# One decode layer on one core: projections with the activations stationary in four column groups, K loaded in 16 KiB runs, layernorm 2 in rows

## The chip, the cores and the metric

The kernel runs on one core of one Trainium2 chip. The metric is the device time of one execution in microseconds (us). Most executions of a kernel agree within 0.3%, so "faster" is kept for more than 2%; smaller differences can still be told apart when several runs agree. "Span" is the time from the first to the last instruction in the profile; the measured time lies about 1.8 us above it, and one section below is about cases where it lies higher. In the views PE is the matmul engine and PEld its weight loads, DVE and ACT are the vector and the scalar engine, and SP issues most of the DMAs. PSUM is the memory that matmuls write to, and an eviction is the copy out of it. "q1", "q8" and "q14" are the DMA queues as the profile numbers them.

## The reference, cut to what matters

Four rows of width 1024 pass through attention over the last 2048 cached keys, and then through a gated feed-forward block.

```python
# B=4 rows, D=1024, Hq=32, Hkv=4, Dh=128, W=2048 keys, F=3584; all bf16
def _A_ref(x, k_cache, v_cache, wq, wo):
    q = (x @ wq) ...                       # wq 1024 x 4096
    scores = einsum("bhqd,bhkd->bhqk", q, k) * Dh ** -0.5
    o = einsum("bhqk,bhkd->bhqd", softmax(scores), v)
    return o ... @ wo                      # wo 4096 x 1024
def _B_ref(x, w1, w3, w2):
    return (silu(x @ w1) * (x @ w3)) @ w2  # w1, w3 1024 x 3584, w2 3584 x 1024
h  = x + _A_ref(_layernorm(x), ...)
h2 = h + _B_ref(_layernorm(h), ...)
```

Each weight and each cached key is read once and used for four rows: 55.6 MB of loads, little arithmetic.

## The kernel before

All loads are issued in the order of use from one queue, into ten buffers of 16 KiB a partition; each buffer is refilled when its tile has been used.

```python
stream = ctx.enter_context(tc.tile_pool(name="stream", bufs=10))
# ... cut ...
def load_kv(cache, b):                      # K and V: runs of 4 KiB
    kv_t = stream.tile([P, Hkv, NK, Dh], BF16, tag="s")
    nc.sync.dma_start(
        out=kv_t[:], in_=cache[b, :, Sk - W : Sk, :].rearrange("g (p j) d -> p g j d", j=NK)
    )
    return kv_t
# ... cut ...
for kc in range(KC):                        # q: the WEIGHTS are stationary, 4 columns stream by
    wq_t = loaded["wq"][kc // KPC]
    for h in range(Hq):
        nc.tensor.matmul(
            qT_ps[:, h, :],
            lhsT=wq_t[:, kc % KPC, h * P : (h + 1) * P],
            rhs=xnT[:, kc, :], ...
        )
    if kc % KPC == KPC - 1:
        load_next()
# ... cut: K transposes, scores, softmax, P times V; wo, gate and up in the same form as q ...
for fc in range(FC):                        # w2: the activations are stationary, four column groups
    w2_t = loaded["w2"][fc // RPC]
    for j in range(JG):
        nc.tensor.matmul(
            y2_ps[32 * j : 32 * j + B, :],
            lhsT=hgT[:, fc, :],
            rhs=w2_t[:, fc % RPC, j * CG : (j + 1) * CG], ...
        )
res = act.tile([P, CG], BF16)
nc.vector.tensor_copy(out=res[:], in_=y2_ps[:])
# ... cut: four small output DMAs, two each from SP and ACT ...
```

The q, wo, gate and up projections need one matmul for each 128 x 128 block of weights: 256 + 256 + 448 of the kernel's 1716 matmuls. Each matmul is two instructions, a weight load and the matmul.

## Time and profile before

| | before |
|---|---|
| time, median of 4 runs | 141.59 us (141.53 to 141.65) |
| span of the profiled run | 139.9 us |
| loads | 55.58 MB, 4096 packets of 4 KiB for K and V |
| matmuls, and as many weight loads | 1716 |
| last load landed / output issued | 136.20 / 137.13 us |

The page of before, cut: the busy share of PE and of the 16 DMA engines in 40 equal slices (in tenths), what they moved, and the DMA queues with packets, MB and share.

```profile
span 139.9 us, 3709 instructions
PE 81.7 (58%) x1716; PEld 66.6 (48%) x1716; DVE 37.0 (26%) x92; ACT 25.4 (18%) x41; POOL 0.7 (1%) x6
...
PE   0252241469999999900897282938966334834460
...
DMA  5999999999999999999999999999999999999930
GB/s 157 426 422 431 436 431 391 425 412 422 422 415 422 422 418 415 421 432 429 429 417 429 426 439 435 419 430 435 418 431 418 443 406 429 417 431 422 405 132 5
...
q1 hardware_dynamic: 8352, 55.58, 95.2%
q8 instruction: 13, 0.21, 0.5%
...
q14 instruction: 2, 0.02, 0.0%
```

The DMA row is full from the second slice to the last but two. No compute stage leaves a dent in it, not even the K stage, where PE is full (slices 10 to 17). With the same bytes to load, two things are left that can shorten this kernel: faster packets, or a shorter way from the last full slice to the end.

The end of the chain of waits before (start, duration, what):

```profile
89.20 32.24 DMA w_t<-in_B_w_dram
121.44 0.02 issue
121.46 14.74 DMA w_t<-in_B_w_dram
136.20 0.04 issue
136.24 0.41 PE y_ps L398 x4
136.66 0.02 issue
136.68 0.42 DVE res L408
```

After the last piece of w2 has landed only 4 matmuls, one eviction and the output follow. Now the load itself, in windows of half a microsecond (the last two columns are the DMA share and GB/s):

```profile
132.00:132.50 0.50, 0.28 (x8) 0.00 (x0) 0.00 (x0) 0.00 (x0) 0.00 (x0) 0.50 1.02 410
132.50:133.00 0.50, 0.00 (x0) 0.00 (x0) 0.00 (x0) 0.00 (x0) 0.00 (x0) 0.50 0.75 303
133.00:133.50 0.50, 0.00 (x0) 0.00 (x0) 0.00 (x0) 0.00 (x0) 0.00 (x0) 0.50 0.59 234
133.50:134.00 0.50, 0.27 (x8) 0.20 (x11) 0.00 (x0) 0.00 (x0) 0.00 (x0) 0.50 0.52 209
134.00:134.50 0.50, 0.50 (x16) 0.31 (x9) 0.00 (x0) 0.00 (x0) 0.00 (x0) 0.50 0.39 156
134.50:135.00 0.50, 0.28 (x12) 0.02 (x7) 0.00 (x0) 0.00 (x0) 0.00 (x0) 0.50 0.33 127
135.00:135.50 0.50, 0.50 (x8) 0.20 (x8) 0.00 (x0) 0.00 (x0) 0.00 (x0) 0.50 0.32 123
135.50:136.00 0.50, 0.46 (x8) 0.09 (x4) 0.00 (x0) 0.00 (x0) 0.00 (x0) 0.50 0.11 41
```

The share does not fall at once, it falls for 3.5 us: the 16 engines do not end together. The trace also holds a completion event for each engine's part of each load. These are the 16 parts of the last load before, in ns after the first of them (which is at 132.9 us):

```
0 37 87 169 211 274 457 | 1239 1379 1726 1837 | 2888 3091 3094 3097 3300
```

Seven engines end together, four about 1.4 us later, five about 1.5 us later still. On the first wq tile the same 16 parts lie within 0.5 us. The page shows what else these engines carry: 13 "instruction" packets on q8, each 16 KiB and 0.88 to 0.96 us long in the trace, against 0.61 us for a 16 KiB packet of data. The trace does not name the engine of a packet or of a part, so which engine carried which packet is inferred from counts and times.

### The profile page before, as it was taken

The numbers are of one execution on the slowest core, as the hardware profiler recorded it, in microseconds if no ns is written. First come the engines' busy times: TensorE is split into PE (matmuls) and PEld (weight loads), VectorE is DVE, ScalarE is ACT, GpSimd is POOL, SyncE is SP. The second block draws the span as 40 slices with busy tenths as digits, with TensorE's granted clock in tenths as the row PEclk, the third lists the DMA queues.
The fourth block names the chain that finished last, engine by engine and source line by source line (L and its number), as shares of the span: only waits on it lengthen the run. The fifth ranks groups of instructions, "written<-read, shape, count | busy, mean of one in ns | idle before, by whom it ended". The sixth has DMA issues, their size and how long they took to land.

```text
span 139.9 us, 3709 instructions
## 1 busy us (share of the span) xinstructions
PE 81.7 (58%) x1716; PEld 66.6 (48%) x1716; DVE 37.0 (26%) x92; ACT 25.4 (18%) x41; POOL 0.7 (1%) x6
## 2 busy tenths in 40 slices
PE   0252241469999999900897282938966334834460
PEld 0252241467777777500797181917966333712120
DVE  6600000335777777661700310012003000000001
ACT  3000000024566666519100000000004000000000
POOL 2000000000000000000000000000000000000000
PEclk9999999999999999997555555555555555555555
DMA  5999999999999999999999999999999999999930
GB/s 157 426 422 431 436 431 391 425 412 422 422 415 422 422 418 415 421 432 429 429 417 429 426 439 435 419 430 435 418 431 418 443 406 429 417 431 422 405 132 5
DMA packets 8391, 55.82 MB, mean 399 GB/s; under 512 B 548, under 2 KB 564, under 8 KB 5048
## 3 DMA queue, kind: packets, MB, share of 16 engines
q1 hardware_dynamic: 8352, 55.58, 95.2%
q8 instruction: 13, 0.21, 0.5%
q10 hardware_dynamic: 24, 0.01, 0.1%
q14 instruction: 2, 0.02, 0.0%
HBM read 55.58 MB, written 0.01 MB: 397 GB/s over the span
## 4 chain that ended last, share of the span: by engine, by line
DMA 52%; PE 32%; DVE 5%; issue 4%; ACT 2%; SPq 1%; ACTq 0%
DMA w_t<-in_B_w_dram 34%; DMA kv_t<-in_A_k_cache_dram 19%; PE kt_ps L232 12%; PE scores_ps L215 10%; PE OT_ps L275 5%; PE yT_ps L313 4%; DVE PT_sb L267 2%; DVE rmax L246 2%; ACT Pm L251 1%; SPq L75 1%; ACT L251 1%; DVE o_1208 L295 1%; PE o_ps L289 0%; PE pt_ps L264 0%; DVE OT_sb L285 0%
## 5 line engine op out<-in xcount | busy, mean ns | idle before, releaser
L236 ACT CAST kT<-kt_ps 128x512 bf16<-128x512 f32 x32 | 17.4, 589 | 37.0 <-PE kt_ps L232 28.0
L234 DVE CAST kT<-kt_ps 128x512 bf16<-128x512 f32 x32 | 20.8, 687 | 10.5 <-ACT kT L236 6.1
L374 PEld LDWEIGHTS <-w_t 128*128 128x128 bf16 x448 | 15.6, 118 | 10.1 <-DMA w_t<-in_B_w_dram 7.9
L232 PEld LDWEIGHTS <-kv_t 128*128 128x128 bf16 x256 | 17.1, 105 | 6.6 <-DMA kv_t<-in_A_k_cache_dram 3.1
L232 PE MATMUL kt_ps<-ident,kv_t 128*128 128x128 bf16 x256 | 18.4, 231 | 3.0 <-DMA kv_t<-in_A_k_cache_dram 3.0
L215 PE MATMUL scores_ps<-kT,Qm 128*128 128x512 bf16 x64 | 17.0, 392 | 0.0
L188 PE MATMUL qT_ps<-xnT,wq_t 128*128 128x4 bf16 x256 | 7.5, 166 | 12.6 <-DMA wq_t<-in_A_wq_dram 12.6
L188 PEld LDWEIGHTS <-wq_t 128*128 128x128 bf16 x256 | 7.1, 104 | 13.0 <-DMA wq_t<-in_A_wq_dram 13.0
L374 PE MATMUL uT_ps<-hnT,w_t 128*128 128x4 bf16 x224 | 8.1, 173 | 7.4 <-DMA w_t<-in_B_w_dram 7.4
L398 PE MATMUL y_ps<-w_t,hgT 128*4 128x256 bf16 x112 | 7.5, 404 | 8.0 <-DMA w_t<-in_B_w_dram 8.0
L313 PE MATMUL yT_ps<-o_1208,wo_t 128*128 128x4 bf16 x256 | 7.2, 166 | 6.5 <-issue 5.1
L313 PEld LDWEIGHTS <-wo_t 128*128 128x128 bf16 x256 | 7.1, 104 | 6.9 <-issue 6.9
L275 PE MATMUL OT_ps<-PT_sb,kv_t 128*128 128x8 bf16 x256 | 7.4, 168 | 2.9 <-issue 2.2
L398 PEld LDWEIGHTS <-hgT 128*4 128x4 bf16 x112 | 3.5, 104 | 11.9 <-issue 10.1
L374 PE MATMUL gT_ps<-hnT,w_t 128*128 128x4 bf16 x224 | 8.0, 173 | 1.8 <-issue 1.3
L275 PEld LDWEIGHTS <-kv_t 128*128 128x128 bf16 x256 | 7.3, 104 | 3.3 <-issue 3.3
L215 PEld LDWEIGHTS <-Qm 128*128 128x128 bf16 x64 | 5.8, 101 | 4.3 <-issue 0.5
L202 DVE TENSOR_SCALAR Qm<-qT_ps 128x8 bf16<-128x8 f32 x16 | 1.3, 158 | 19.9 <-PE qT_ps L188 19.9
L264 PE MATMUL pt_ps<-Dm,Pm 128*128 128x128 bf16 x16 | 1.9, 311 | 6.6 <-DVE Dm L257 6.6
L345 ACT ACTIVATE rstd_t<-var_t,eps_t 128x4 f32<-128x4 f32 x1 | 0.3, 297 | 28.4 <-DVE var_t L343 28.4
L264 PEld LDWEIGHTS <-Pm 128*128 128x128 bf16 x16 | 1.6, 146 | 7.0 <-ACT Pm L251 7.0
L408 DVE CAST res<-y_ps 128x256 bf16<-128x256 f32 x1 | 0.4, 425 | 15.3 <-PE y_ps L398 15.3
(58 smaller groups left out, 30.1 us busy)
## 6 DMA issues: line engine op xcount, KB each, us to landing
w_t<-in_B_w_dram SPq DMA_DIRECT2D x8, 1792.0 KB, 31.9
wq_t<-in_A_wq_dram SPq DMA_DIRECT2D x4, 2048.0 KB, 7.3
kv_t<-in_A_k_cache_dram SPq DMA_DIRECT2D x4, 2048.0 KB, 32.9
kv_t<-in_A_v_cache_dram SPq DMA_DIRECT2D x4, 2048.0 KB, 23.6
wo_t<-in_A_wo_dram SPq DMA_DIRECT2D x4, 2048.0 KB, 24.3
w_t<-in_B_w_dram SPq DMA_DIRECT2D x6, 1024.0 KB, 27.7
w_t<-in_B_w_dram SPq DMA_DIRECT2D x1, 512.0 KB, 20.1
w_t<-in_B_w_dram SPq DMA_DIRECT2D x2, 256.0 KB, 14.7
```

Of the source, the lines that this page charges most:

```text
L188: nc.tensor.matmul(qT_ps[:, h, :], lhsT=wq_t[:, kc % KPC, h * P : (h + 1) * P], rhs=xnT[:, kc, :], start=(kc == 0 and h == 0), stop=(kc == ...
L215: nc.tensor.matmul(scores_ps[:, n * 512 : (n + 1) * 512], lhsT=Qm[:, bg2, :], rhs=kT_tiles[bg2][:, n * 4 : (n + 1) * 4, :], start=(bg2 == ...
L232: nc.tensor.matmul(kt_ps[:, jj, :], lhsT=k_t[:, g, j, :], rhs=ident[:], start=True, stop=True)
L234: nc.vector.tensor_copy(out=kT[:, jb * JPB : (jb + 1) * JPB, :], in_=kt_ps[:])
L236: nc.scalar.copy(out=kT[:, jb * JPB : (jb + 1) * JPB, :], in_=kt_ps[:])
L246: nc.vector.reduce_max(out=rmax[:], in_=scores_ps[:], axis=AX.X)
L251: nc.scalar.activation(out=Pm[:], in_=scores_ps[:], func=ACT.Exp, bias=nmax[:], scale=1.0, accum_out=rsum[:],)
L264: nc.tensor.matmul(pt_ps[:, jj, :], lhsT=Pm[:, j * P : (j + 1) * P], rhs=Dm[:], start=True, stop=True)
L275: nc.tensor.matmul(OT_ps[:, b, g * REP : (g + 1) * REP], lhsT=v_t[:, g, j, :], rhs=PT_sb[:, j, b * Hq + g * REP : b * Hq + (g + 1) * REP], ...
L313: nc.tensor.matmul(yT_ps[:, dc, :], lhsT=wo_r[:, dc // KPC, dc % KPC, :], rhs=o4[:, h4, r, :], start=(h4 == 0 and r == 0 and dc == 0), sto ...
L374: nc.tensor.matmul(gu_ps[i][:, fc, :], lhsT=w_v[:, fc // RPC, fc % RPC, :], rhs=hnT[:, kc, :], start=(kc == 0 and fc == 0), stop=(kc == KC ...
L398: nc.tensor.matmul(y2_ps[32 * j : 32 * j + B, :], lhsT=hgT[:, fc, :], rhs=w2_t[:, fc % RPC, j * CG : (j + 1) * CG], start=False, stop=(fc ...
```

## The change

The intent was to make PE's work smaller. The four rows of activations become the stationary operand in all projections, the weights stream past, and four column groups of PE work side by side, as in w2 before. For the scores the same is done by head, which asks for K with the heads interleaved over partitions; this gives K runs of 16 KiB. Layernorm 2 moves to the row layout that the new projections leave. The core of the diff (cuts marked):

```diff
-    def load_kv(cache, b):
+    def load_k(b):
+        k_t = stream.tile([P, JK * Dh], BF16, tag="s")
         nc.sync.dma_start(
+            out=k_t[:],
+            in_=A_k_cache[b, :, Sk - W : Sk, :].rearrange("g (pp j) d -> pp g (j d)", pp=PK),
 ... (V stays in runs of 4 KiB; w2 now in tiles of 7 rows, loaded in pieces of 4 and 3)
+    x_q = act.tile([P, CG], BF16)
+    for j in range(JG):
+        nc.scalar.dma_start(
+            out=x_q[QD * j : QD * j + B, :], in_=x_flat[:, j * CG : (j + 1) * CG]
+        )
 ...
-            nc.tensor.matmul(
-                qT_ps[:, h, :],
-                lhsT=wq_t[:, kc % KPC, h * P : (h + 1) * P],
-                rhs=xnT[:, kc, :],
+        for hf in range(CQ // 512):
+            for g in range(JG):
+                c0 = g * CQ + hf * 512
+                nc.tensor.matmul(
+                    q_ps[QD * g : QD * g + B, hf * 512 : (hf + 1) * 512],
+                    lhsT=xnT[:, kc, :],
+                    rhs=wq_t[:, kc % KPC, c0 : c0 + 512],
 ... (wo, gate and up likewise; K by transposes into bf16; scores by head in 32 columns;
      layernorm 2 by statistics of 256 columns, joined by one small matmul; gate over 896 columns)
     res = act.tile([P, CG], BF16)
-    nc.vector.tensor_copy(out=res[:], in_=y2_ps[:])
+    nc.vector.tensor_copy(out=res[:, : CG // 2], in_=y2_ps[:, : CG // 2])
+    nc.scalar.copy(out=res[:, CG // 2 :], in_=y2_ps[:, CG // 2 :])
```

## The prediction

> **What bounds it now.** The 16 DMA engines. The 40 slices show DMA at 9 tenths from slice 2 to the end of slice 38, about 424 GB/s, and the queue table 55.58 MB. The windows view shows no dip in the K phase (413 to 423 GB/s, 26 to 61 us), although PE is the chain there: ten buffers hide it. From 102 us on, every weight tile is waited for (wait view: PE waits 15.5 us for w_t). The chain ends in the last w2 piece, landing at 136.2; then 4 matmuls 0.41, eviction 0.42, output to 139.9.
>
> **The end is ragged.** In the windows view the DMA share falls to 0.75, 0.59, 0.52, 0.39, 0.33, 0.32, 0.11 in half-microsecond steps from 132.5 on. The completion events say why: the 16 parts of one load land 0.5 us apart at first, and 3.3 us apart at the end, in three groups: seven engines 0 to 0.4 us, four 1.2 to 1.9, five 2.9 to 3.3. The groups grow one by one with the 13 instruction packets (queue q8: 16 KiB each, about 0.94 us). A ninth packet, at 97 us, starts the third group: so they look dealt in turn over eight engines, five of which got two. The Trainium skill (DMA: Bandwidth & Descriptors, Queues, rings and completion order) says that each engine goes round between the queues it has work for; the trace agrees, at about 1.4 us lost per packet.
>
> **What the change does.**
> 1. PE instructions. Matmuls fall from 1716 to about 1055 (q 256 to 64, wo 256 to 128, gate and up 448 to 128; K transposes, scores, V, w2 keep their counts), each with a weight load. 3432 instructions for 13 packets is 264 each; 2110 give an estimated 8 packets: no engine should get two. Worth one step of the ragged end: -1.4 us (range 0 to 1.7). On the critical path, because the last load waits for its slowest engine.
> 2. K in 16 KiB runs: 2048 packets of 4 KiB become 512. Packets took 159 ns (4 KiB), 309 (8), 611 (16); landings of 2 MiB tiles were 4.97, 4.90 and 4.86 us apart. Four tiles: -0.45 us, on the path. w2 rows of 8 and 6 KiB cost an estimated +0.05 us.
> 3. Eviction split over DVE and ACT: -0.13 us of 0.42.
> 4. Four extra small x loads: +0.1 us.
> 5. Off the path: the projections (column groups already run side by side: 112 w2 matmuls of 404 ns take 7.5 us), scores with 32 columns, bigger K evictions, row layernorm. They end attention earlier, but the DMA was never starved, so I count 0. The gate's reciprocal grows from 112 to 896 elements a row: 0.85 us to an estimated 6.5, hidden beneath w3's 17 us.
>
> Sum: 141.61 - 1.4 - 0.45 - 0.13 + 0.15 = **139.8 us**; range 138.8 to 141.3. Faster by over 2% (below 138.8): 0.1; within 2%: 0.87; slower: 0.03.
>
> **What would show it.** About 8 instruction packets on q8; last parts at most about 2 us apart instead of 3.3; the DMA share falling over 2 us rather than 3.5; last w2 landing near 134.4. K packets of 16 KiB near 611 ns, tiles 4.86 us apart. PE busy falls a lot and PE's idle time grows by as much. Last wait before the output still DMA.
>
> **What would make it wrong.** Packets dealt otherwise, so that one engine still gets two (then 141). K runs 2 MB apart in a partition's neighbours hitting memory worse than 4 KiB runs (up to +1). Switching between full and column-group matmuls, or strided reads of kT, stretching K by over 10 us, so that buffers come free late and the DMA starves: then slower. Chain at the gate not hidden: +1.

## The result, and the profile after

Before took 141.59 us and after 139.99 us (medians of 4 runs, after from 139.94 to 140.57). The ratio is 0.9897, with a 95% interval from 0.987 to 0.9923. Ratios here are the mean time of one kernel's fast runs over that of the other's of the same rounds, so not quite the ratio of the medians. By the 2% rule this is "the same", but the 1.6 us are well outside the scatter of before.

The page of after, the same lines:

```profile
span 138.2 us, 2365 instructions
PE 75.0 (54%) x1057; PEld 43.4 (31%) x1057; DVE 37.1 (27%) x71; ACT 29.4 (21%) x29; POOL 0.7 (1%) x6
...
DMA  5999999999999999999999999999999999999950
GB/s 154 433 423 436 417 436 436 441 413 432 441 402 409 420 421 416 425 423 430 429 429 417 425 442 424 428 432 428 432 428 432 432 432 413 421 427 430 409 216 2
...
q1 hardware_dynamic: 6960, 55.58, 95.7%
q8 instruction: 8, 0.13, 0.3%
...
q14 instruction: 1, 0.01, 0.0%
```

The end of the chain of waits after:

```profile
121.33 12.97 DMA w_t<-in_B_w_dram
134.29 0.04 issue
134.34 0.41 PE y_ps L448 x4
134.75 0.02 issue
134.77 0.30 DVE res L458
135.07 0.02 issue
135.10 0.27 ACT res L459
```

And the windows at the end of the load:

```profile
131.50:132.00 0.50, 0.15 (x4) 0.10 (x7) 0.00 (x0) 0.00 (x0) 0.00 (x0) 0.50 1.09 434
132.00:132.50 0.50, 0.50 (x12) 0.26 (x5) 0.00 (x0) 0.00 (x0) 0.00 (x0) 0.50 0.87 344
132.50:133.00 0.50, 0.16 (x4) 0.00 (x0) 0.00 (x0) 0.00 (x0) 0.00 (x0) 0.50 0.57 221
133.00:133.50 0.50, 0.42 (x8) 0.23 (x8) 0.00 (x0) 0.00 (x0) 0.00 (x0) 0.50 0.58 221
133.50:134.00 0.50, 0.47 (x8) 0.09 (x4) 0.00 (x0) 0.00 (x0) 0.00 (x0) 0.50 0.28 107
```

The middle of the DMA row is as full as before. The fall at the end takes 2 us instead of 3.5, and the chain says where the time went: the last load lands at 134.29 instead of 136.20 us, 1.91 us earlier, and about 0.17 us are given back between the end of the last matmuls and the output, which was issued at 135.39 us (135.39 - 134.75 = 0.64 us; before 137.13 - 136.66 = 0.47). Together that is the 1.7 us by which the span is shorter. The 16 parts of the last load (the first at 132.46 us):

```
0 90 180 253 346 391 428 | 1175 1480 1489 1562 1572 1716 1783 1809 1840
```

The third group is gone. The first engines end 0.4 us earlier than before (132.46 against 132.9), the last ones 1.9 us earlier. These are two effects, and the experiments take them apart.

### The profile page after: what moved, and what is told of

Read it like the earlier page. It is cut to its first block, busy times and chain, and to the rows that moved or that the text cites. A ratio compares the mean times of both kernels' runs of the same rounds, so it can differ in the third digit from the quotient of the medians.

```text
span 138.2 us, 2365 instructions
## 1 busy us (share of the span) xinstructions
PE 75.0 (54%) x1057; PEld 43.4 (31%) x1057; DVE 37.1 (27%) x71; ACT 29.4 (21%) x29; POOL 0.7 (1%) x6
## 4 chain that ended last, share of the span: by engine, by line
DMA 74%; PE 16%; ACT 5%; SPq 1%; issue 1%; DVE 0%; ACTq 0%
DMA w_t<-in_B_w_dram 55%; DMA k_t<-in_A_k_cache_dram 14%; PE kt_ps L271 10%; DMA wq_t<-in_A_wq_dram 5%; ACT kT L277 5%; PE scores_ps L256 5%; SPq L118 1%; PE y_ps L448 0%; DVE res L458 0%; ACT res L459 0%; SPq L111 0%; ACTq L277 0%
## 5 line engine op out<-in xcount | busy, mean ns | idle before, releaser
L277 ACT COPY kT<-kt_ps 128x1024 bf16<-128x1024 bf16 x16 | 15.9, 1013 | 14.5 <-PE kt_ps L271 14.5
L271 PE MATMUL kt_ps<-ident,k_t 128*128 128x128 bf16 x256 | 18.0, 231 | 0.9 <-DMA k_t<-in_A_k_cache_dram 0.9
L271 PEld LDWEIGHTS <-k_t 128*128 128x128 bf16 x256 | 15.9, 104 | 6.1 <-issue 4.9
L275 DVE COPY kT<-kt_ps 128x1024 bf16<-128x1024 bf16 x16 | 11.1, 692 | 17.6 <-PE kt_ps L271 17.6
L223 PE MATMUL q_ps<-wq_t,xnT 128*4 128x512 bf16 x64 | 7.5, 620 | 11.2 <-DMA wq_t<-in_A_wq_dram 11.2
L414 PE MATMUL u_ps<-w_t,hnT 128*4 128x448 bf16 x64 | 6.7, 567 | 10.3 <-DMA w_t<-in_B_w_dram 10.3
L256 PE MATMUL scores_ps<-kT,qz 128*32 128x512 bf16 x64 | 9.9, 609 | 3.0 <-ACT kT L277 3.0
L414 PE MATMUL g_ps<-w_t,hnT 128*4 128x448 bf16 x64 | 6.5, 570 | 5.0 <-DMA w_t<-in_B_w_dram 4.7
L323 PE MATMUL OT_ps<-PT_sb,v_t 128*128 128x8 bf16 x256 | 7.4, 168 | 1.7 <-issue 1.4
L323 PEld LDWEIGHTS <-v_t 128*128 128x128 bf16 x256 | 7.3, 104 | 1.9 <-issue 1.7
```

The costliest lines, as they stand in the source:

```text
L223: nc.tensor.matmul(q_ps[QD * g : QD * g + B, hf * 512 : (hf + 1) * 512], lhsT=xnT[:, kc, :], rhs=wq_t[:, kc % KPC, c0 : c0 + 512], start=( ...
L256: nc.tensor.matmul(scores_ps[QD * g : QD * (g + 1), n * 512 : (n + 1) * 512], lhsT=qz[:, b, g * QD : (g + 1) * QD], rhs=kT_v[:, g, :, :], ...
L271: nc.tensor.transpose(out=kt_ps[:, jj, :], in_=k_v[:, n * NJ + t * TB + jj, :], identity=ident[:])
L275: nc.vector.tensor_copy(out=kT[:, t * TB : (t + 1) * TB, :], in_=kt_ps[:])
L277: nc.scalar.copy(out=kT[:, t * TB : (t + 1) * TB, :], in_=kt_ps[:])
L323: nc.tensor.matmul(OT_ps[:, b, g * REP : (g + 1) * REP], lhsT=v_t[:, g, j, :], rhs=PT_sb[:, j, g * QD + b * REP : g * QD + (b + 1) * REP], ...
```

## The experiments

**My theory.** Two small things shorten the kernel, both in the DMA engines. (a) PE's instructions come through the same 16 engines, in packets of 16 KiB that are dealt in turn to eight of them. A packet holds up the data of its engine by about 1.4 us. The last load waits for the engine that got most of them, so the time has steps: none, one, two packets on one engine. Before had 13 packets, so five engines got two; after has 8. (b) K in 16 KiB runs saves packets. The time of PE's work itself counts nothing.

**Rivals.** That the whole gain is the K layout. That shorter PE work or an earlier end of attention gained. That instruction packets count only by their mean share: 5 packets fewer, 0.94 us each, over 16 engines are 0.3 us.

All numbers of one group ran on the same chip with their own runs of before. The wrong kernels leave out or misplace part of the attention or feed-forward sums. The check of results nevertheless passed all of them but the last: x dominates the output. So that check says little about these sums, in any of the kernels here.

### Each part alone: before_trim and before_k16k

In before_trim, every second term of the sums is left out (the same edit in P times V and wo):

```diff
-        for h in range(Hq):
+        for h in range(Hq if kc % 2 == 0 else 0):
...
-            for fc in range(FC):
+            for fc in range(FC if kc % 2 == 0 else 0):
```

> The kernel before with every second accumulation term left out in q, P times V, wo, gate and up (result wrong on purpose; all loads, K work and evictions stay), so PE has about 2190 instructions instead of 3432. Theory of dealt instruction packets: 8 packets instead of 13, no DMA engine gets two, parts of the last load land under 2 us apart, 1.4 us less than before: near 140.2 us. Rival, only the mean DMA work counts (5 packets of 0.94 us over 16 engines): 0.3 us less, near 141.3 us. Rival, gain of the change lies in the K layout and the softmax alone: 141.6 us.

Measured: 140.17 us against 141.58 us for before, 1.41 us less (ratio 0.9901). The page has 8 packets on q8, and the windows fall as in after:

```profile
133.00:133.50 0.50, 0.24 (x8) 0.04 (x7) 0.00 (x0) 0.00 (x0) 0.00 (x0) 0.50 0.59 229
133.50:134.00 0.50, 0.50 (x8) 0.19 (x8) 0.00 (x0) 0.00 (x0) 0.00 (x0) 0.50 0.56 213
134.00:134.50 0.50, 0.44 (x8) 0.09 (x4) 0.00 (x0) 0.00 (x0) 0.00 (x0) 0.50 0.15 57
```

The parts of the last load make two groups of 7 and 9; the first lands at 132.86 us (before: 132.9), the last at 134.66 (136.2). The loads are untouched, so the K layout is not the whole gain, and the mean of the packets is too small by more than a factor of four.

In before_k16k only the K load changes:

```diff
+    def load_k(cache, b):
+        k_t = stream.tile([P, Hkv, NK, Dh], BF16, tag="s")
+        nc.sync.dma_start(
+            out=k_t[:].rearrange("p g j d -> p (g j d)"),
+            in_=cache[b, :, Sk - W : Sk, :].rearrange("g (pp j) d -> pp g (j d)", pp=P // Hkv),
+        )
```

> The kernel before with only the K load in 16 KiB runs (result wrong on purpose). Theory: 0.45 us less than before, near 141.15 us, and the ragged end stays: parts of the last load still land over 3 us apart, since PE still has 13 instruction packets. Rival, K layout is the whole gain: 140.0 us.

Measured: 141.02 us, 0.56 us less than before (ratio 0.996, 0.9948 to 0.9972). The parts keep three groups of 7, 4 and 5, ending 3.07 us apart; all of them come earlier (first at 132.46 instead of 132.9). That is effect (b), alone.

The two single effects add to 1.97 us. After gained 1.60.

### K back to 4 KiB in the kernel after: after_k4k

```diff
-            out=k_t[:],
-            in_=A_k_cache[b, :, Sk - W : Sk, :].rearrange("g (pp j) d -> pp g (j d)", pp=PK),
+            out=k_t[:].rearrange("p (g m) -> p g m", g=Hkv),
+            in_=A_k_cache[b, :, Sk - W : Sk, :].rearrange("g (p j) d -> p g (j d)", j=NK),
```

> The kernel after with only the K load put back to 4 KiB runs (the heads then lie wrongly: the result is wrong on purpose, the instructions stay). Theory of packets: K tiles land 4.97 us apart instead of 4.87, four of them: 0.45 us more than after, near 140.4 us. Rival, that long runs matter nothing when the engines are busy anyway: no change, 140.0 us. Rival, that the K layout is the whole gain: 141.6 us.

Measured: 140.75 us (140.42 to 141.07), 0.76 us above the 139.99 of after, more than expected. But after was timed on another occasion, and both kernels scatter by 0.6 us. The spans scatter less: 138.5 us (138.4 to 138.6) against 138.1 (138.0 to 138.2), 0.4 us; and the first part of the last load lands 0.5 us later. So the K runs are worth about 0.4 to 0.55 us both ways. The scatter had to be explained otherwise; see the eviction below.

### Instruction packets put back: after_pad9, after_pad13, after_pad17

Tiny matmuls are added where PE waits for wq (and for 13 packets also behind each w1 and w3 tile). They write to an unused buffer, so the result stays right.

```diff
         if kc % KPC == KPC - 1:
             load_next()
+            for _ in range(50):
+                nc.tensor.matmul(idle_ps[:4, :4], lhsT=xnT[:, 0, :], rhs=xnT[:, 0, :], start=True, stop=True)
```

> The kernel after with 200 tiny matmuls (4 rows by 4 columns, into an unused buffer, result still right) put where PE waits for wq, 50 after each of the four tiles. PE has about 2510 instructions instead of 2114: 9 instruction packets, so one engine gets a second one. Theory: the slowest engine decides, so this ninth packet alone costs a whole step: 1.4 us more than after, near 141.4 us, parts of the last load over 3 us apart with a single part in the third group. Rival, mean DMA work: 0.06 us more. Rival, shorter PE work is what gained: no change, as PE was idle there.

Measured: 141.59 us, exactly the time of before on that chip (141.59; ratio 1.0, 0.9988 to 1.0013). By the spans, 139.3 us against 138.1 for after: 1.2 us. The page shows 10 packets on q8 rather than 9; the tenth came only at 134.0 us, when 12 of the 16 parts of the last load had landed. The parts of the last load:

```
0 7 72 211 220 322 394 | 1236 1419 1450 1460 1502 1637 1665 1837 | 2937
```

This fits a single engine with a second packet, whose part alone sets the time: the chain ends in the last load, as in after, with its landing at 135.43 us. The windows show it as a long thin tail:

```profile
133.50:134.00 0.50, 0.30 (x8) 0.00 (x1) 0.00 (x0) 0.00 (x0) 0.00 (x0) 0.50 0.27 102
134.00:134.50 0.50, 0.31 (x8) 0.23 (x8) 0.00 (x0) 0.00 (x0) 0.00 (x0) 0.50 0.18 57
134.50:135.00 0.50, 0.45 (x12) 0.09 (x4) 0.00 (x0) 0.00 (x0) 0.00 (x0) 0.50 0.07 29
135.00:135.50 0.50, 0.24 (x8) 0.02 (x3) 0.00 (x0) 0.00 (x0) 0.00 (x0) 0.50 0.01 4
```

> The same with 720 tiny matmuls, 80 after each wq tile and 50 after each w1 and w3 tile: about 3550 PE instructions, 13 packets as in the kernel before. Theory: no more than with 9 packets, as no engine gets three: 1.4 us more than after, near 141.4 us, five parts in the third group. Rival, each packet costs the same: 5 times the cost of the ninth.

Measured: 141.90 us, span 139.5: the further 520 tiny matmuls cost 0.2 us of span over after_pad9. The q8 count is 14, the last of them only at 134.3 us, when 11 of the 16 parts had landed, and the parts make groups of 7, 4 and 5, as before had them. So from the ninth to the thirteenth packet there is almost nothing more to pay: steps, not a slope.

> The same with 1280 tiny matmuls (100 after each wq tile, 70 after each batch of V, 75 after each w1 and w3 tile): about 4670 PE instructions, 17 packets, so one engine gets a third. Theory: a second step, 2.8 us more than after, near 142.8 us, one part of the last load alone in a fourth group, over 4 us after the first.

Measured: 159.45 us. This run failed as a test. 1280 tiny matmuls were too much for PE: it came late to everything, and the chain to the end is PE's, with evictions by ACT and DVE between. The timeline of its PE after the load was over:

```profile
135.57 5.18 PE L422 MATMUL u_ps<-w_t,hnT 128*4 128x448 bf16 x64
146.99 0.95 PE L447 MATMUL hg_ps<-ident,hg 128*128 128x128 bf16 x7 [6.24 <-DVE hg L442]
148.25 5.64 PE L458 MATMUL y_ps<-w_t,hgT 128*4 128x256 bf16 x112 [0.31 <-DVE hgT L449]
```

The loads had ended at 135.5 us. Only 16 packets had come by 132.0 us, and the parts make groups of 7, 1 and 8, as if every one of eight engines had exactly two. This fits the dealing in turn, but a third step was not seen and stays untested.

### Still fewer instructions: after_trim4

```diff
-            for j in range(NK):
+            for j in range(0, NK, 4):
...
-            for r in range(KPC):
+            for r in range(1):
```

(and half of the terms in q and wo)

> The kernel after with terms left out (three of four in P times V, half in q, wo, gate and up; result wrong on purpose): about 1400 PE instructions, 5 packets. Theory: one packet on one engine is already the first step, so going from 8 to 5 gains nothing: within 0.3 us of after, 140.0 us, parts of the last load still about 1.8 us apart. Rival, gain in proportion to the PE instructions: 0.8 us less, near 139.2 us.

Measured: 140.23 us (139.9 to 140.45), span 138.0 us against 138.1 for after. The page has 5 packets on q8 and 705 matmuls instead of 1057, PE is busy 58.8 us instead of 75.0, and nothing is gained. The parts make groups of 10 and 6, ending 1.6 us apart. The sixth is the one 8 KiB packet on q14 at about 59 us: it too seems to put an engine into the second group. This run also rules out PE's work as the source of the gain.

The groups in one table; "first" and "last" are the parts of the last load in us of the span:

| kernel | matmuls | q8 packets before the load's end | parts in groups | first | last | span |
|---|---|---|---|---|---|---|
| before | 1716 | 13 | 7, 4, 5 | 132.9 | 136.2 | 139.9 |
| before_k16k | 1716 | 13 | 7, 4, 5 | 132.46 | 135.52 | 139.2 |
| before_trim | 1108 | 8 | 7, 9 | 132.86 | 134.66 | 138.4 |
| after | 1057 | 8 | 7, 9 | 132.46 | 134.29 | 138.2 |
| after_k4k | 1057 | 8 | 7, 9 | 132.97 | 134.64 | 138.5 |
| after_trim4 | 705 | 5 | 10, 6 | 132.56 | 134.16 | 138.0 |
| after_pad9 | 1257 | 9 | 7, 8, 1 | 132.50 | 135.43 | 139.3 |
| after_pad13 | 1777 | 13 | 7, 4, 5 | 132.45 | 135.65 | 139.5 |

The "first" column moves with the K layout, the gap from first to last with the packets, both but for small rests: with 13 packets the gap is 3.07 to 3.3 us, with 8 it is 1.8. With n packets dealt in turn over eight engines, and the q14 packet on a ninth, each row's groups come out right.

The steps also show within one run. In before, the second, third and fourth wq tile are first used at 12.97, 19.38 and 24.25 us: the third comes 6.41 us after the second, the fourth 4.87 us after the third. The first instruction packet had started at 16.8 us. The ninth started at 97.0 us, and the last part of the last w1 tile landed at 102.05 us, 5.78 us after that of the tile before it; the other w1 and w3 tiles follow each other by 4.24 to 4.28 us. Of the 13 packets only the first and the ninth, one for each new group, delayed a landing so.

### The eviction: after_1evict, after_1evict_2, after_actevict, after_again

```diff
-    nc.vector.tensor_copy(out=res[:, : CG // 2], in_=y2_ps[:, : CG // 2])
-    nc.scalar.copy(out=res[:, CG // 2 :], in_=y2_ps[:, CG // 2 :])
+    nc.vector.tensor_copy(out=res[:], in_=y2_ps[:])
```

> The kernel after with one eviction of the result by DVE, as before had it. In the trace after, the two halves run one after the other (DVE 0.30 us, then ACT 0.27 us, the output issued 0.64 us after the last matmuls; before 0.45 us). If the split is a loss: 0.2 us less than after, near 139.8 us, output issue about 0.45 us after the last matmuls. If the split is the gain that the prediction counted: about 0.1 us more than after.

Measured: 139.83 us (139.78 to 139.92), ratio to before 0.9878. To compare it with after fairly, both were run again on one chip, with a third kernel in which ACT alone evicts.

> The kernel after itself, as a control on the chip of the next three. In all runs so far with the split eviction, the time lies 1.85 to 2.47 us above the span of the profile; in all without it (before, its two variants, after with one eviction) 1.75 to 1.9. Expected: span 138.1, time between 139.95 and 140.6 us, scattered.

> The kernel after with one eviction by DVE, again, beside the kernel after. If the split causes both the 0.2 us in the span and the scatter above the span: span 138.0, time 139.8 us with all runs within 0.15 us, and less than after on the same chip by 0.2 to 0.5 us. If the scatter was of the chip or the job: no difference from after in scatter.

> The kernel after with the whole eviction on ACT, none on DVE. If an ACT copy just before ACT issues output is what adds the time above the span: 1.85 to 2.45 us above the span here too. If it is the hand-over from DVE to ACT: 1.8 us above the span, time near 139.8 us.

| same chip | time, us | span | time above the span |
|---|---|---|---|
| after_again (split) | 140.50 (140.04 to 140.55) | 138.2 | 1.94 to 2.38 |
| after_1evict_2 (DVE) | 139.81 (139.68 to 139.88) | 138.0 | 1.78 to 1.88 |
| after_actevict (ACT) | 140.28 (140.13 to 140.55) | 138.1 | 2.15 to 2.35 |

The control came out 0.5 us above the first median of after: the first one's runs lay mostly in the lower part of the scatter. The timeline of after_again shows the end of the span:

```profile
134.91 0.29 DVE L458 CAST res<-y_ps 128x128 bf16<-128x128 f32 x1 [13.64 <-PE y_ps L448]
135.24 0.27 ACT L459 CAST res<-y_ps 128x128 bf16<-128x128 f32 x1 [31.03 <-DVE res L458]
135.53 0.67 SPq L462 DMA_DIRECT2D out_dram<-res  x2
```

and of after_1evict_2:

```profile
134.74 0.42 DVE L458 CAST res<-y_ps 128x256 bf16<-128x256 f32 x1 [13.59 <-PE y_ps L448]
135.19 0.66 SPq L461 DMA_DIRECT2D out_dram<-res  x2
```

The halves did not run side by side. ACT waited for DVE, 0.62 us from DVE's start to the output instead of 0.45. The Trainium skill (PSUM — Partial Sum Buffer, PSUM bank collisions raise a hardware error) says that two engines on one bank and quadrant at once is an error and must be kept apart. Both halves of this tile, 1 KiB a partition together, fit into one bank (2 KiB a partition in the same page's Specifications (TRN2)); the trace agrees in that ACT starts only 0.04 us after DVE has ended. But the bank cannot be the whole reason. The kernel after splits one more eviction, that of q, and there each half takes 2 KiB a partition, so that the halves lie in two banks. They ran in series all the same:

```profile
24.58 0.69 DVE L233 TENSOR_SCALAR q_sb<-q_ps 128x512 bf16<-128x512 f32 x1 [16.95 <-PE q_ps L223]
25.30 0.60 ACT L234 ACTIVATE q_sb<-q_ps 128x512 bf16<-128x512 f32 x1 [20.90 <-DVE q_sb L233]
```

Evictions from two different PSUM tiles did overlap: of P transposed, DVE copied from 66.93 to 67.62 us and ACT from 67.36 to 67.95, into one tile. So the record shows that halves of one PSUM tile waited for each other; why they do so even in two banks stays open.

The second cost lies outside the span. In all kernels in which ACT copies just before it issues its output (split or alone), the time lies 1.85 to 2.47 us above the span; in all others 1.75 to 1.9. So the expectation that the hand-over was to blame has fallen: after_actevict has no hand-over and the same excess. What happens in this excess stays open. The traces hold one clue that no experiment followed. In the traces of all eight runs with an ACT copy at the end, an 8 KiB instruction packet on q14 starts 2.09 to 2.12 us after the end of the span. The three runs in which DVE alone evicts for after (after_1evict, after_1evict_2, after_noxq) have none there, and before and its two variants have theirs 0.5 to 0.8 us before the end of the span. So the excess may be a wait for one more fetch of instructions rather than for the copy as such; this is not tested. Together the split costs 0.7 us on this chip (140.50 - 139.81), of 1.7 us that the rest of the change gains.

### The four small loads of x: after_noxq

```diff
-    for j in range(JG):
-        nc.scalar.dma_start(
-            out=x_q[QD * j : QD * j + B, :], in_=x_flat[:, j * CG : (j + 1) * CG]
-        )
```

(on top of one eviction; the result is wrong)

> The kernel after with one eviction and without the four small loads of x by quarters (x is then missing from the sum: wrong on purpose). The prediction counted 0.1 us for them. Theory: within 0.1 us of the kernel with one eviction, since the first wq tile lands at 8.1 us in the kernels before and after alike. Rival, the small packets delay the engines that end last: 0.2 us or more less.

Measured: 139.73 us against 139.81 for after_1evict_2 on the same chip, 0.08 us, within the scatter of either. These loads cost at most 0.1 us.

## Why the prediction was right or wrong

The time was right: 139.8 us predicted, 139.99 measured, in the range. The steps, as the prediction put them:

1. **PE instructions, -1.4 us: right.** The packets fell from 13 to 8 as worked out, the third group vanished, and doing this alone in before_trim gave -1.41 us. The step from 8 to 9 packets costs 1.2 us of span, and from 9 to 13 only 0.2 more. The Trainium skill (DMA: Bandwidth & Descriptors, Queues, rings and completion order) says that each engine goes round between the queues it has work for; the groups fit that, at 1.2 to 1.5 us lost for one packet, but no trace shows the turns themselves. The loss is more than the 0.94 us the packet takes, and why is open.
2. **K runs, -0.45 us: right.** before_k16k gave -0.56 us, after_k4k +0.4 us of span. K tiles landed about 4.87 us apart instead of 4.97. The packet durations alone, 32 of 159 ns against 8 of 611 ns per engine and tile, would give 5.09 and 4.89 us; packets of 4 KiB overlap a little, so the landings are the better measure.
3. **"Eviction split over DVE and ACT: -0.13 us of 0.42": wrong.** It cost 0.17 us inside the span, as the halves ran in series, and up to 0.5 us more above it, which no view of before could have shown. The prediction assumed that two engines may read one PSUM tile together. That the halves of one tile ran in series shows in both split evictions of after; the reason is not shown. In the first result this miss was half hidden, by luck, as three of the four runs had little of the excess: the same kernel took 140.50 us as after_again, 0.7 us above the prediction.
4. **x loads, +0.1 us: right** within what can be measured (0.08).
5. **Off the path, 0: right in time.** No slice of DMA is less full than before; after_trim4 took away 16 us of PE work and gained nothing. The reciprocal took 5.75 us instead of the estimated 6.5, hidden under w3. But "PE busy falls a lot" was wrong: it fell only from 81.7 to 75.0 us; what fell is weight loading, from 66.6 to 43.4. Matmuls with four stationary columns stream the whole weight, so as many instructions fewer are not as much time less: the q matmuls took 7.5 us as 256 before and 7.5 us as 64 after.

So the sum came out close because a miss of 0.3 us on the eviction stood against effects that were each as large as predicted or slightly larger (1.41 and 0.56 alone). They do not quite add: after with one eviction gains 1.72 us on its chip, not 1.97. Most of the rest lies in the gap of the last load, which the K runs alone shortened from 3.3 to 3.07 us in before, while after has the same 1.8 us as before_trim. Of the two kernels, neither is the best: after with one eviction by DVE takes 139.81 to 139.83 us, ratio 0.9875 to before (0.9862 to 0.9889), and changes nothing in the result's arithmetic.

## What to carry to other kernels

When the DMA engines are full from end to end, look at how they end: the completion events of the last load tell whether all engines end together, and the slowest one sets the time. Instructions are loads too, and they come in steps: shortening a straight-line program helps when it takes the fullest engine's count down by one, and not otherwise (13 to 8 packets gained 1.4 us, 8 to 5 nothing). Before a short eviction is split over two engines, look in the trace whether two such halves overlap at all: halves of one PSUM tile did not here, in one bank or in two, and evictions of different PSUM tiles did. And time it, since part of its cost may lie outside the span.

## What the Trainium skill lacked or had wrong

- Runtime: NRT & Kernel Launch, Instruction fetch mechanics, has the refill in blocks of 16 KiB or 256 instructions, which agrees: 1410, 2114, 2216, 2514, 3432, 3554 and 4674 matmul and weight-load instructions gave 5, 8, 8, 10, 13, 14 and 18 packets of 16 KiB on q8, near one for each 256. (The prediction counted 264, so after_pad9 and after_pad13 got one packet more than expected.) It calls the cost of crossing a block "mostly hidden". In this kernel, bound by DMA, it is not: parts of the last load come 1.2 to 1.5 us later in each further group, and the ninth packet alone lengthened the span by 1.2 us.
- No page says how these packets are spread. Here PE's came on q8, and the completion events fit dealing in turn over eight of the 16 engines (groups of 7, 8 and 1 with nine packets; 7, 4 and 5 with 13).
- DMA: Bandwidth & Descriptors, Queues, rings and completion order, puts refill on queue row 14. If the profile's q numbers are those rows, PE's refill is not there: its 16 KiB packets were on q8, and q14 carried one 8 KiB instruction packet in the middle of the run (at 52.2 us in before, 58.9 us in after) and, in most kernels, one more near or after the end of the span.
- No page tells of the excess above the span with a copy by ACT just before the end of a program: 0.1 to 0.5 us more in the runs of after_again and after_actevict than with DVE, 0.35 us by the medians. Its cause is open.
